# A fused retention and two-MLP kernel on one core: k and v of the first chunks on ScalarE's DMA queue, head and visits reordered, outputs in the next first bank

## The chip, the cores and the metric

The kernel runs on one core of one Trainium2 chip. A core has a matrix engine (TensorE, PE in the rows; its weight loads are PEld), a vector engine (VectorE, DVE), an activation engine (ScalarE, ACT), GpSimd (POOL) and SyncE (SP), which here does nothing but issue DMAs. Every engine works through its own list of instructions in order and waits on semaphores for the others. ScalarE can issue DMAs too. Data come from device memory into SBUF (128 partitions); matmuls write PSUM banks, which VectorE and ScalarE read. The metric is device time in microseconds, taken as the median of several runs. A profiled execution gives a span, from its first to its last instruction.

## The reference

Three stages on 4 sequences of 576 tokens, 8 heads of 64: a retention (attention without softmax, with a decay by head), then a softplus MLP and a squared-ReLU MLP, both 512 to 2048 to 512.

```
scores = (1/sqrt(D)) * q @ k^T
gamma  = 1 - 2.0 ** (-5 - arange(H))
ret    = scores * where(rel >= 0, gamma ** rel, 0)      # rel = i - j
x      = (ret @ v) -> [B*S, H*D]                         # 2304 x 512
h = x @ w_in;  g = max(h,0) + log1p(exp(-|h|));  x = g @ w_out
h = x @ w_in2; r = max(h,0); g = r*r;            out = g @ w_out2
```

All of it is float32.

## The kernel before, in words

**Retention by chunks.** The tokens are cut into 18 chunks of 64 positions of two sequences each (128 tokens). A chunk has one SBUF tile `ch`: its lower 64 partitions hold q and k by dimension, its upper 64 hold k and v by token, so each chunk comes in by transfers that write 64 partitions each (`load_chunk`). For a chunk, `scale_v` weights v with the decay. `step_s` then runs 32 matmuls for the scores (`pb`) and, interleaved, 32 for the running state (`st`), VectorE masks the scores back into `ch` (L355), and ScalarE copies the state into the next chunk's tile (L362). `step_o` runs 32 matmuls for the output (`po`), and VectorE multiplies it with weights `xw` into x (L393). For the first token tile ScalarE rounds x to `xh` (L400) and VectorE takes the rest `xl` (L401), since float32 matmuls are made of rounded parts: `ph` sums xh·wi and xl·wi.

**The MLPs.** Tokens go in five tiles (`TILES`, 512, 384, 512, 512, 384). A tile has 16 steps: g1 (12 matmuls into `ph`, L446), the softplus on ScalarE and VectorE (last line L473), and two steps later g2 (12 matmuls into `acc`, L498). `ph` alternates between two PSUM banks. Weights arrive as raw words through three staging buffers and are converted by ScalarE (L142, L143, L175) and VectorE (L147, L176) during the first tile. The later chunks of the retention are done in *visits* between steps (`attend`): output of chunk c−1, load of chunk c+1, scores and state of chunk c, scale of chunk c+1. In a visit before the change `po` has a bank of its own, and `pb` is put into the bank that the next `ph` takes. The second MLP (L592, L611) follows on six accumulators a batch, whose results are stored by two DMAs each, lower and upper partitions apart (L510).

**What sets the order.** The head, up to the first MLP, is in the order in which it is written (`tc.manual_schedule()`): loads first, then chunk by chunk, with dummy matmuls (`cold`, `keep_warm`) between. After it a scheduler merges the work of steps, visits and conversions, so the order on each engine is seen only in its list. All input DMAs stand on SP.

Of the kernel before, what the change touches and what calls it, by code (L numbers as in the profile page):

```python
# [43 lines left out]
def kernel(  # L44
# [74 lines left out]
    def load_w(src, kind, f):  # L119
        t = stage.tile([P, DM, 2], U32, tag="st", name=f"{kind}_raw")  # L120
        if kind == "wi":
            nc.sync.dma_start(
                out=t.rearrange("p (k m) two -> p k (m two)", k=KD),
                in_=src[:, f * P:(f + 1) * P].rearrange("(k p) m two -> p k (m two)", p=P),
            )
        else:
            nc.sync.dma_start(out=t, in_=src[f * P:(f + 1) * P])
# [114 lines left out]
    def pump_load(upto):  # L242
        while n_load[0] < min(upto, len(loads)):
            load_w(*loads[n_load[0]])
            n_load[0] += 1
# [52 lines left out]
    def new_chunk(c):  # L298
        if c < NPR:
            pool = first_pool if c < n_first else at  # L300
            chunk[c] = pool.tile([P, 3, 2, H, CN], F32, tag="ch", name="ch")

    def load_qk(c):
        if c < NPR:
            if c not in chunk:
                new_chunk(c)
            for s in range(2):
                nc.sync.dma_start(out=chunk[c][LO, 0:2, s], in_=qk_t[place(c, s)])

    def load_kv(c):  # L310
        if c < NPR:
            for s in range(2):
                nc.sync.dma_start(out=chunk[c][HI, 1:3, s], in_=kv[place(c, s)])

    def load_chunk(c):
        load_qk(c)
        load_kv(c)

    def scale_v(c, eng=nc.vector):
        if c < NPR:  # L320
            t = chunk[c][HI, 2]
            w = cst[HI, C_VW + c % SCH * H:C_VW + (c % SCH + 1) * H]
            eng.tensor_tensor(  # L323
                out=t, in0=t, op=ALU.mult,
                in1=w.unsqueeze(1).unsqueeze(3).to_broadcast([CN, 2, H, D]),
            )
# [7 lines left out]
    def step_s(c, pb):  # L334

        qp, kk, sv = (chunk[c][:, i] for i in range(3))
# [23 lines left out]
        if go_on:  # L360
            for of, i in ((LO, 0), (HI, 1)):
                nc.scalar.copy(chunk[c + 1][LO, 2, :, i * HH:(i + 1) * HH], st[of])  # L362

    def pb_acc():
        return ps_acc.tile([P, H, CN], F32, tag="at", name="pb")

    def step_o(c, ps):
        qkv = chunk.pop(c)
        qp, sv = qkv[:, 0], qkv[:, 2]
        rows = slice(0, P) if c % SCH else HI  # L370
        xw = xw_first if c % SCH == 0 else xw_now
        xw = xw.rearrange("p (a b) -> p a b", a=KD).unsqueeze(1).to_broadcast([P, 2, KD, CN])
        po = ps.tile([P, H, CN], F32, tag="at", name="po").rearrange(
            "p (s a) b -> p s a b", s=2
        )
        if c % SCH:
            make_xw(c % SCH)
# [54 lines left out]
    def pb_next():  # L432
        return h_bank("pb", False).rearrange("p (h c) -> p h c", c=CN)
# [68 lines left out]
    def drain_one(j, src, dsts, n):  # L502
# [6 lines left out]
        for rows, dst in dsts:  # L509
            nc.sync.dma_start(out=dst, in_=o[rows])  # L510
# [216 lines left out]
    nc.scalar.preload_act_table_set("natural_log_exp_and_others")  # L727
# [29 lines left out]
    def make_xw(m):  # L757
# [3 lines left out]
            out=xw_now.rearrange("p (a b) -> p a b", a=KD),  # L761
# [5 lines left out]
    with tc.manual_schedule():  # L767
# [24 lines left out]
        for c in range(last + 1):  # L792
            scale_v(c, nc.vector if c == last - 1 else nc.gpsimd)
            if c < last:
                keep_warm(1)
                step_s(c, pb_acc())
                if c:
                    step_o(c - 1, ps_acc)
                for _ in range((0, 0, 1, 2)[c]):
                    pump_step()  # L800
# [5 lines left out]
    step_s(last, pb_acc())  # L806
    tick[0] = last + 1
# [141 lines left out]
```

## Time and profile before

| what | us |
|---|---|
| median of 3 runs (885.42 to 886.35) | 885.65 |
| profiled execution, own time | 886.12 |
| its span | 884.4 |
| TensorE busy | 848.1 (96%) |
| VectorE busy | 577.6 (65%) |
| ScalarE busy | 421.8 (48%) |
| mean granted TensorE clock | 0.979 |

The time is a little longer than the span, since starting and ending lie outside of it. TensorE is busy 96% of the span, so the kernel is bound by it over most of its length; a share over the whole span says nothing on the stages at its two ends, where TensorE waits. In the page's rows a group reads: line, engine, operation, output from input, count, then busy time, mean of one, and the idle time just before with what ended it.

### The profile page before, as it was taken

The page shows a single profiled execution, that of the slowest core. Times are in us where ns is not written, and L with a number is a line of the kernel's source. Part 1 is how long each engine was busy: PE and PEld are TensorE (multiplying, and loading weights), DVE is VectorE, ACT ScalarE, POOL GpSimd, SP SyncE. Part 2 cuts the span into 40 slices and gives each one's busy share as a digit, 9 for nine tenths or more (in the row PEclk, how much of TensorE's full clock was granted, in tenths as well). Part 3 has the DMA queues.
Part 4 walks back from the last instruction along what each step waited for, and adds up shares of the span by engine and source line. Part 5 has one row for each costly group of instructions (what it writes and reads, how often), then busy time and mean ns, then how long its engine had stood idle before and what let it go on. Part 6 is the DMA issues. An engine that isn't in the chain of part 4 may idle for free.

```text
span 884.4 us, 14178 instructions
## 1 busy us (share of the span) xinstructions
PE 848.1 (96%) x5512; PEld 744.7 (84%) x5512; DVE 577.6 (65%) x974; ACT 421.8 (48%) x759; POOL 8.2 (1%) x8
## 2 busy tenths in 40 slices
PE   6699989999999999999999999999999999999996
PEld 5678778899877888788999989889888889998885
DVE  1689889886798668854888874547644445544543
ACT  2579889675577445744686461213322113221121
POOL 2100000000000000000000000000000000000000
PEclk7799999999999999999999999999999999999999
DMA  9776685883288106900431374346644344634343
GB/s 194 179 205 198 175 179 161 234 267 109 49 239 239 41 8 176 311 2 1 163 118 54 124 237 118 117 120 190 190 116 116 115 120 119 191 119 110 118 119 72
DMA packets 80678, 126.32 MB, mean 143 GB/s; under 512 B 7010, under 2 KB 41954, under 8 KB 80610
## 3 DMA queue, kind: packets, MB, share of 16 engines
q1 hardware_dynamic: 80612, 125.42, 50.9%
q8 instruction: 44, 0.72, 0.3%
q14 instruction: 22, 0.18, 0.1%
HBM read 101.28 MB, written 24.12 MB: 142 GB/s over the span
## 4 chain that ended last, share of the span: by engine, by line
PE 65%; DMA 12%; DVE 12%; ACT 7%; issue 2%; SPq 2%; DVEq 0%; ACTq 0%
PE acc L611 22%; PE ph L446 12%; PE acc L498 9%; PE py L592 8%; DMA ch<-in_kv_dram 7%; PE px L592 6%; PE pz L592 6%; DMA wi_raw<-in_moe_w_in_dram 3%; DMA wo_raw<-in_moe_w_out_dram 2%; DVE ct L147 2%; DVE e L473 1%; DVE l L470 1%; DVE e L467 1%; DVE ch L323 1%; DVE ch L355 1%
## 5 line engine op out<-in xcount | busy, mean ns | idle before, releaser
L446 PE MATMUL ph<-xh,wi 128*128 128x512 f32 (+1 forms) x640 | 152.1, 380 | 12.3 <-DVE ch L355 6.2
L446 PEld LDWEIGHTS ph<-xh,wi 128*128 128x128 f32 x640 | 118.6, 193 | 34.3 <-issue 5.0
L498 PE MATMUL acc<-gh,woh 128*128 128x512 f32 (+1 forms) x320 | 118.7, 372 | 0.0
L498 PE MATMUL acc<-gl,woh 128*128 128x512 f32 (+1 forms) x320 | 117.9, 368 | 0.0
L498 PE MATMUL acc<-gh,wol 128*128 128x512 f32 (+1 forms) x320 | 117.8, 368 | 0.0
L611 PE MATMUL acc<-woh,gring 128*128 128x512 f32 x288 | 104.9, 393 | 0.0
L592 PE MATMUL py<-t,sring 128*128 128x384 f32 x432 | 86.9, 335 | 0.3 <-DVE uring L703 0.3
L482 ACT CAST gh<-e 128x512 fp32r<-128x512 f32 (+1 forms) x80 | 46.0, 575 | 78.6 <-DVE e L473 72.5
L592 PEld LDWEIGHTS py<-t,sring 128*128 128x128 f32 x432 | 77.2, 188 | 6.8 <-DVE uring L703 0.6
L446 PE MATMUL ph<-xl,wi 128*128 128x512 f32 (+1 forms) x320 | 79.5, 369 | 0.0
L467 DVE SCALAR_TENSOR_TENSOR e<-e 128x512 f32<-128x512 f32 (+1 forms) x80 | 50.9, 636 | 37.4 <-ACT l L462 36.8
L483 DVE TENSOR_TENSOR gl<-e,gh 128x512 fp32r<-128x512 f32 (+1 forms) x80 | 50.9, 636 | 27.6 <-ACT gh L482 27.4
L498 PEld LDWEIGHTS acc<-gh,woh 128*128 128x128 f32 x320 | 60.0, 188 | 8.1
L498 PEld LDWEIGHTS acc<-gl,woh 128*128 128x128 f32 x320 | 60.1, 188 | 7.7 <-DVE gl L483 0.3
L498 PEld LDWEIGHTS acc<-gh,wol 128*128 128x128 f32 x320 | 60.1, 188 | 7.7
L446 PEld LDWEIGHTS ph<-xl,wi 128*128 128x128 f32 x320 | 59.5, 190 | 8.1
L641 ACT CAST gh<-g 128x384 fp32r<-128x384 f32 x48 | 24.6, 513 | 87.3 <-DVE g L628 72.6
L641 ACT CAST gring<-g 128x384 fp32r<-128x384 f32 x48 | 24.6, 513 | 80.1 <-DVE g L628 80.1
L460 ACT ACTIVATE e<-ph 128x512 f32<-128x512 f32 (+1 forms) x80 | 44.1, 552 | 38.6 <-PE ph L446 38.3
L611 PEld LDWEIGHTS acc<-woh,gring 128*128 128x128 f32 x288 | 54.0, 188 | 9.2
L592 PE MATMUL px<-t,sring 128*128 128x384 f32 x288 | 58.4, 337 | 0.0
L592 PE MATMUL pz<-t,sring 128*128 128x384 f32 x288 | 58.2, 337 | 0.0
(80 smaller groups left out, 1427.3 us busy)
## 6 DMA issues: line engine op xcount, KB each, us to landing
sring<-s2d SPq DMA_DIRECT2D x168, 256.0 KB, 2.7
wi_raw<-in_moe_w_in_dram SPq DMA_DIRECT2D x32, 512.0 KB, 4.8
wo_raw<-in_moe_w_out_dram SPq DMA_DIRECT2D x32, 512.0 KB, 4.6
s2d<-ct SPq DMA_DIRECT2D x48, 256.0 KB, 3.3
ch<-in_qk_t_dram SPq DMA_DIRECT2D x36, 256.0 KB, 4.9
ch<-in_kv_dram SPq DMA_DIRECT2D x36, 256.0 KB, 6.0
raw<-x2d SPq DMA_DIRECT2D x12, 384.0 KB, 3.4
out_dram<-xo SPq DMA_DIRECT2D x36, 128.0 KB, 2.4
```

The source lines that it names most:

```text
L147: nc.vector.scalar_tensor_tensor(out=ct, in0=up, scalar=3, in1=low, op0=ALU.logical_shift_left, op1=ALU.bitwise_or,)
L323: eng.tensor_tensor(out=t, in0=t, op=ALU.mult, in1=w.unsqueeze(1).unsqueeze(3).to_broadcast([CN, 2, H, D]),)
L355: nc.vector.tensor_tensor(out=qp[HI, :, i * HH:(i + 1) * HH], in0=pb[of].rearrange("p (s h) c -> p s h c", s=2), in1=mask[of].rearrange("p ...
L446: nc.tensor.matmul(ph[:, :n], lhsT=a, rhs=x, start=(j == 0), stop=(j == len(todo) - 1))
L460: nc.scalar.activation(out=e, in_=ph[:, :n], func=AF.Abs)
L467: nc.vector.scalar_tensor_tensor(out=e, in0=e, scalar=-2.0, in1=e, op0=ALU.add, op1=ALU.mult)
L482: nc.scalar.copy(h[:, :n], g)
L483: nc.vector.tensor_tensor(out=l[:, :n], in0=g, in1=h[:, :n], op=ALU.subtract)
L498: nc.tensor.matmul(acc[j][:, :n], lhsT=a, rhs=x, start=(begin and m == 0), stop=(end and m == 2))
L592: nc.tensor.matmul(ps, lhsT=a, rhs=x, start=(first and m == 0), stop=(m == len(todo) - 1), skip_group_check=True,)
L611: nc.tensor.matmul(acc2[j, m], lhsT=a, rhs=x, start=(begin and n == 0), stop=(end and n == 2))
L641: nc.scalar.copy(h, g)
```

## The change

1. *Queues in the head.* `load_w`, `pump_load` and `load_chunk` can issue on another queue. k and v of chunks 0 to 3 and the first weight block are issued by ScalarE, the rest of the head by SP. The table load of ScalarE moves behind its first DMA.
2. *Chunk tile.* It is laid out sequence by sequence, so one DMA brings q and k (or k and v) of both sequences, 512 KB, in pieces of 4 KB; before, two DMAs of 256 KB in pieces of 2 KB.
3. *Order in the head.* The weight blocks are loaded ahead of chunk 4; GpSimd scales all five of the head's chunks, in two instructions each; the output weights of chunks 1 to 3 are made early (`xw_soon`); the state copies become a call of their own (`next_state`); chunk 4's `step_s` moves into the first visits, of which the first tile now has four.
4. *Visits.* Scores first, into the bank that `po` had; the output of the chunk before goes into the bank of the next `ph` (`in_next`).
5. *Outputs.* The two stores of a result go one on SP and one on ScalarE.

```diff
+    def load_chunk(c, kv_queue=nc.sync):
...
+            at_c = slice(place(c, 0), place(c, 1) + 1, SCH)
+            nc.sync.dma_start(
+                out=chunk[c][LO, :, 0:2], in_=qk_t[at_c].rearrange("s p i h c -> p s i h c")
+            )
+            kv_queue.dma_start(
+                out=chunk[c][HI, :, 1:3], in_=kv[at_c].rearrange("s p i h c -> p s i h c")
+            )
...
-        for rows, dst in dsts:
-            nc.sync.dma_start(out=dst, in_=o[rows])
+        for queue, (rows, dst) in zip((nc.sync, nc.scalar), dsts):
+            queue.dma_start(out=dst, in_=o[rows])
...
-        load_chunk(0)
+        load_chunk(0, nc.scalar)
+        nc.scalar.preload_act_table_set("natural_log_exp_and_others")
...
-        for c in range(1, last + 1):
-            load_chunk(c)
-            if c == last - 2:
-                pump_load(1)
-            elif c == last - 1:
-                pump_load(3)
+        load_chunk(1, nc.scalar)
+        pump_load(1, nc.scalar)
+        load_chunk(2, nc.scalar)
+        load_chunk(3, nc.scalar)
+        pump_load(3)
+        load_chunk(last)
...
+        for c in range(last):
+            scale_v(c, nc.gpsimd)
+            keep_warm(2)
+            step_s(c, in_acc("pb"))
+            next_state(c)
+            if c:
+                step_o(c - 1, in_acc("po"))
+            for _ in range((0, 1, 2, 0)[c]):
+                pump_step()
         keep_warm(2)
-        step_o(last - 1, ps_acc)
-        keep_warm(6)
+        step_o(last - 1, in_acc("po"))
+        keep_warm(4)
+        scale_v(last, nc.gpsimd)
...
+            if b == 0:
+                before, n = before - 1, n + 1
...
                 c = tick[0]
-                step_o(c - 1, ps_at)
+                if c < NPR:
+                    step_s(c, ps_at.tile([P, H, CN], F32, tag="at", name="pb"))
+                if c - 1 in chunk:
+                    step_o(c - 1, in_next("po"))
                 load_chunk(c - 1 + LOADS)
                 if c < NPR:
-                    step_s(c, pb_next())
+                    next_state(c)
                 scale_v(c - 1 + LOADS)
```

What moves, engine by engine. First the loads of the head. On SP before, the first twelve transfers after the constants' rows (`ch` is a chunk, `cst` the masks and decay weights; L308 loads q and k, L313 k and v):

```order
L308 DMA ch<-in_qk_t_dram 64x2x512 x2
L313 DMA ch<-in_kv_dram 64x2x512 x2
L776 DMA cst<-in_consts_dram 64x138 x2
L308 DMA ch<-in_qk_t_dram 64x2x512 [waits DMAHW0_49]
L308 DMA ch<-in_qk_t_dram 64x2x512 [waits DMAHW1_49]
L313 DMA ch<-in_kv_dram 64x2x512 [waits DMAHW2_49]
L313 DMA ch<-in_kv_dram 64x2x512 [waits DMAHW3_49]
```

On SP now, up to chunk 4 (L308 q and k, L311 k and v, L122 a weight block):

```order
L308 DMA ch<-in_qk_t_dram 64x2x1024
L781 DMA cst<-in_consts_dram 64x138 x2
L308 DMA ch<-in_qk_t_dram 64x2x1024 [waits DMAHW0_49]
L308 DMA ch<-in_qk_t_dram 64x2x1024 [waits DMAHW2_49]
L308 DMA ch<-in_qk_t_dram 64x2x1024 [waits DMAHW4_49]
L122 DMA wi_raw<-in_moe_w_in_dram 128x4x256 [waits DMAHW5_49]
L122 DMA wi_raw<-in_moe_w_in_dram 128x4x256 [waits DMAHW6_49]
L308 DMA ch<-in_qk_t_dram 64x2x1024 [waits DMAHW7_49]
L311 DMA ch<-in_kv_dram 64x2x1024 [waits DMAHW0_49]
```

And on ScalarE now, from its start; before, its first row was the table load and its second the copy of the constants' rows:

```order
L311 DMA ch<-in_kv_dram 64x2x1024
L779 ACT_TABLE_LOAD
L311 DMA ch<-in_kv_dram 64x2x1024
L122 DMA wi_raw<-in_moe_w_in_dram 128x4x256
L311 DMA ch<-in_kv_dram 64x2x1024 [waits DMAHW1_49]
L311 DMA ch<-in_kv_dram 64x2x1024 [waits DMAHW3_49]
L757 COPY cst<-rows 128x256 [waits PE_49]
L361 COPY ch<-st 64x2x256 [waits PE_49]
```

The upper halves of chunks 0 to 3 left SP's list. A DMA that waits for a DMA semaphore waits for the landing of the last transfer that used it, which can be one of the other queue.

Second, VectorE ahead of the first `ph` (`ct` and `wi` are weight conversions, `ch<-pb` a mask, `x<-po` the output product). Before, from the `xl` of chunk 2:

```order
L401 TENSOR_TENSOR xl<-x,xh 128x2x4x64 [waits Activation_49]
L147 SCALAR_TENSOR_TENSOR ct<-wi_raw 128x512 [waits DMAHW0_49]
L147 SCALAR_TENSOR_TENSOR ct<-wi_raw 128x512 [waits DMAHW5_49]
L147 SCALAR_TENSOR_TENSOR ct<-wi_raw 128x512 [waits DMAHW6_49]
L176 TENSOR_TENSOR wi_393<-ct,wi_393 128x512 [waits Activation_49]
L760 SCALAR_TENSOR_TENSOR xw_now<-cst 128x256
L355 TENSOR_TENSOR ch<-pb,cst 64x2x256 [waits PE_49]
L393 TENSOR_TENSOR x<-po,xw_now 128x512 [waits DVE_49]
L355 TENSOR_TENSOR ch<-pb,cst 64x2x256
```

Now, from the `xl` of chunk 1 to the x of chunk 3:

```order
L404 TENSOR_TENSOR xl<-x,xh 128x2x4x64 [waits Activation_49]
L147 SCALAR_TENSOR_TENSOR ct<-wi_raw 128x512 [waits DMAHW6_49]
L147 SCALAR_TENSOR_TENSOR ct<-wi_raw 128x512 [waits DMAHW5_49]
L147 SCALAR_TENSOR_TENSOR ct<-wi_raw 128x512 [waits DMAHW6_49,Activation_49]
L176 TENSOR_TENSOR wi_331<-ct,wi_331 128x512 [waits Activation_49]
L352 TENSOR_TENSOR ch<-pb,cst 64x2x256 [waits PE_49]
L352 TENSOR_TENSOR ch<-pb,cst 64x2x256
L396 TENSOR_TENSOR x<-po,xw_soon 128x512 [waits PE_49]
L176 TENSOR_TENSOR wi_331<-ct,wi_331 128x512 [waits Activation_49] x2
L404 TENSOR_TENSOR xl<-x,xh 128x2x4x64 [waits Activation_49]
L396 TENSOR_TENSOR x<-po,xw_soon 128x512 [waits PE_49]
```

The masks here were chunk 4's and are now chunk 3's; chunk 4's come behind. On TensorE chunk 4's state matmuls still stand ahead of the first `ph`, but no longer its output matmuls.

Third, a visit in the second tile, on VectorE (`xr` is x of a later tile, `gl` and `e` softplus, the 128x256 `ct` a weight conversion). Before:

```order
L393 TENSOR_TENSOR xr<-po,xw_now 128x512 [waits PE_49]
L483 TENSOR_TENSOR gl<-e,gh 128x384 [waits Activation_49]
L467 SCALAR_TENSOR_TENSOR e<-e 128x384 [waits Activation_49]
L210 TENSOR_TENSOR ct<-ct 128x256 [waits DVE_49]
L470 SCALAR_TENSOR_TENSOR l<-e,l 128x384 [waits DVE_49]
L355 TENSOR_TENSOR ch<-pb,cst 64x2x256 [waits PE_49]
L355 TENSOR_TENSOR ch<-pb,cst 64x2x256
L473 SCALAR_TENSOR_TENSOR e<-ph,l 128x384 [waits DVE_49]
```

Now:

```order
L185 TENSOR_TENSOR ct<-ct 128x512 [waits DMAHW2_49,Activation_49]
L352 TENSOR_TENSOR ch<-pb,cst 64x2x256 [waits PE_49]
L352 TENSOR_TENSOR ch<-pb,cst 64x2x256
L396 TENSOR_TENSOR xr<-po,xw_now 128x512 [waits PE_49]
L470 SCALAR_TENSOR_TENSOR e<-e 128x384 [waits Activation_49]
L185 TENSOR_TENSOR ct<-ct 128x512 [waits DMAHW4_49,Activation_49]
```

The two masks stand ahead of the output's product, with nothing between; what is last of a visit to leave the next `ph`'s bank is the product and not the masks.

## Rows read from the trace of the kernel before

**Rows 1.** Five stages: busy time by engine, then clock, DMA share, GB/s.

```profile
0.00:44.29 44.29, 29.90 (x530) 26.49 (x530) 18.94 (x28) 16.11 (x28) 8.16 (x8) 0.74 0.85 186
44.29:148.50 104.21, 98.06 (x623) 78.45 (x623) 88.63 (x141) 90.23 (x159) 0.00 (x0) 0.95 0.71 188
148.50:500.00 351.50, 343.43 (x2492) 302.33 (x2491) 268.49 (x453) 217.64 (x389) 0.00 (x0) 1.00 0.44 129
500.00:876.30 376.30, 376.01 (x1869) 337.23 (x1868) 200.76 (x355) 97.28 (x185) 0.00 (x0) 1.00 0.48 137
876.30:884.40 8.10, 0.68 (x4) 0.22 (x2) 0.74 (x2) 0.59 (x1) 0.00 (x0) 0.81 0.74 170
```

**Rows 2.** Chain of waits through the head: start us, us, what.

```profile
17.99 15.43 DMA wi_raw<-in_moe_w_in_dram
...
36.51 0.69 DVE xl L401
37.20 3.52 DVE ct L147 x3
...
44.36 4.91 PE ph L446 x12
```

**Rows 3.** DMA issues of the first 40 us: count, KB, us to landing.

```profile
ch<-in_qk_t_dram SPq DMA_DIRECT2D x12, 256.0 KB, 7.7
ch<-in_kv_dram SPq DMA_DIRECT2D x10, 256.0 KB, 8.4
wi_raw<-in_moe_w_in_dram SPq DMA_DIRECT2D x3, 512.0 KB, 14.3
```

**Rows 4.** Stretches with different transfers, columns as in rows 1.

```profile
3.50:4.00 0.50, 0.50 (x5) 0.50 (x4) 0.00 (x0) 0.00 (x0) 0.00 (x0) 1.00 1.13 401
...
12.00:17.00 5.00, 3.56 (x89) 3.02 (x92) 1.38 (x2) 1.16 (x2) 1.90 (x1) 0.50 1.07 212
...
26.00:28.00 2.00, 0.00 (x0) 0.00 (x0) 0.69 (x1) 1.64 (x3) 0.00 (x0) 1.00 1.08 326
...
47.00:50.00 3.00, 3.00 (x29) 2.26 (x27) 0.69 (x1) 0.67 (x3) 0.00 (x0) 0.75 1.06 373
```

**Rows 5.** Timeline of the head: scales on GpSimd, first state matmuls of two chunks.

```profile
9.89 1.90 POOL L323 TENSOR_TENSOR ch<-ch,cst 64x1024 f32<-64x1024 f32 x1 [9.45 <-DMA cst<-in_consts_dram]
...
11.85 0.37 PE L350 MATMUL st<-ch 64*64 64x64 f32 x2 [5.02 <-POOL ch L323]
...
16.40 0.37 PE L350 MATMUL st<-ch 64*64 64x64 f32 x2 [1.44 <-POOL ch L323]
...
36.72 2.25 POOL L323 TENSOR_TENSOR ch<-ch,cst 64x1024 f32<-64x1024 f32 x1 [15.45 <-DMA ch<-in_kv_dram]
```

**Rows 6.** Waits after 44 us: us in total, times, longest.

```profile
ACT wo_raw L142 <- DMA wo_raw<-in_moe_w_out_dram: 12.9, 10, 3.5
...
PE ph L446 <- DVE ch L355: 6.2, 8, 1.2
PE ph L446 <- DVE e L473: 6.0, 5, 2.6
```

**Rows 7.** The tail: stretch, store issues, the last copy, landing times.

```profile
876.00:882.00 6.00, 0.98 (x5) 0.48 (x3) 1.04 (x2) 0.59 (x1) 0.00 (x0) 0.95 0.89 206
...
874.23 7.54 SPq L510 DMA_DIRECT2D out_dram<-xo  x12
...
878.53 0.69 DVE L508 COPY xo<-acc 128x512 f32<-128x512 f32 x1 [2.18 <-DMA out_dram<-xo]
...
out_dram<-xo SPq DMA_DIRECT2D x12, 128.0 KB, 2.4
```

**Rows 8.** First middle group of stores: a cast, its matmul; the ring's loads.

```profile
631.47 0.51 ACT L641 CAST gh<-g 128x384 fp32r<-128x384 f32 x1 [0.17 <-DVE g L628]
...
632.25 0.39 PE L611 MATMUL acc<-woh,gh 128*128 128x512 f32 x1
...
sring<-s2d SPq DMA_DIRECT2D x168, 256.0 KB, 2.7
```

More of the change, by code (lines that the diff above doesn't have):

```diff
@@ L126, in load_w @@
         else:
-            nc.sync.dma_start(out=t, in_=src[f * P:(f + 1) * P])
+            queue.dma_start(out=t, in_=src[f * P:(f + 1) * P])
         staged[kind, f] = t
@@ L240, with pump_load @@
     n_used = [0]
-    def pump_load(upto):
+    def pump_load(upto, queue=nc.sync):
         while n_load[0] < min(upto, len(loads)):
-            load_w(*loads[n_load[0]])
+            load_w(*loads[n_load[0]], queue)
             n_load[0] += 1
@@ L300, in new_chunk @@
             pool = first_pool if c < n_first else at
-            chunk[c] = pool.tile([P, 3, 2, H, CN], F32, tag="ch", name="ch")
-    def load_qk(c):
+            chunk[c] = pool.tile([P, 2, 3, H, CN], F32, tag="ch", name="ch")
+    def load_chunk(c, kv_queue=nc.sync):
         if c < NPR:
@@ L306, in load_qk @@
                 new_chunk(c)
[L307 to L317, printed above, removed]
+            at_c = slice(place(c, 0), place(c, 1) + 1, SCH)
[5 more added lines that the diff above has]
+            )
     def scale_v(c, eng=nc.vector):
         if c < NPR:
-            t = chunk[c][HI, 2]
             w = cst[HI, C_VW + c % SCH * H:C_VW + (c % SCH + 1) * H]
[L323 to L326, printed above, removed]
+            for s in range(2) if eng is nc.gpsimd else (slice(0, 2),):
+                t = chunk[c][HI, s, 2]
+                w_s = w.unsqueeze(2)
+                if len(t.shape) == 4:
+                    w_s = w_s.unsqueeze(1)
+                eng.tensor_tensor(out=t, in0=t, in1=w_s.to_broadcast(list(t.shape)), op=ALU.mult)
     state = []
@@ L334, in step_s @@
     def step_s(c, pb):
-        qp, kk, sv = (chunk[c][:, i] for i in range(3))
+        qp, kk, sv = (chunk[c][:, :, i] for i in range(3))
         go_on = c % SCH < SCH - 1
@@ L359, in step_s, with next_state, in_acc, step_o @@
             )
-        if go_on:
+    def next_state(c):
+        if c % SCH < SCH - 1:
             for of, i in ((LO, 0), (HI, 1)):
[L362 to L367, printed above, removed]
+                nc.scalar.copy(
+                    chunk[c + 1][LO, :, 2, i * HH:(i + 1) * HH], state[0][of]
+                )
+    def in_acc(name):
+        return ps_acc.tile([P, H, CN], F32, tag="at", name=name)
+    def step_o(c, po):
         qkv = chunk.pop(c)
-        qp, sv = qkv[:, 0], qkv[:, 2]
+        qp, sv = qkv[:, :, 0], qkv[:, :, 2]
         rows = slice(0, P) if c % SCH else HI
-        xw = xw_first if c % SCH == 0 else xw_now
-        xw = xw.rearrange("p (a b) -> p a b", a=KD).unsqueeze(1).to_broadcast([P, 2, KD, CN])
[L373 to L377, printed above, removed]
+        if c % SCH == 0:
+            xw = xw_first
+        elif c < n_first:
+            xw = xw_soon[:, c - 1]
+        else:
+            xw = xw_now
+            make_xw(xw, c % SCH)
+        xw = xw.rearrange("p (a b) -> p a b", a=KD).unsqueeze(1).to_broadcast([P, 2, KD, CN])
+        po = po.rearrange("p (s a) b -> p s a b", s=2)
         for s in range(2):
@@ L839 @@
         softplus_a(j, n)
-        if j == 0:
-            for c in range(last + 1, last + LOADS):
-                load_chunk(c)
-                scale_v(c)
         if j >= 1:
```

28 lines of the change are left out of this document (10 added, 18 removed).

## Prediction

> **What bounds the kernel now.** I read the table of stages first, then the chain of waits, then the DMA views. [rows 1] cut the span at four moments: the first matmul of the first MLP (44.29 us), the end of its first tile (148.5), the start of the second MLP (500), and the last matmul (876.3). From 500 on TensorE is busy 376.01 of 376.3 us, and from 148.5 to 500 all but 8: nothing is to be won there except at waits. What is left is the head (44.29 us, TensorE busy 29.90, much of it warm-up matmuls and half clock), the first tile (idle 6.15 of 104.21) and a tail of 8.1 us without matmuls.
>
> The chain through the head [rows 2] is DMA up to 33.42 (the last piece alone begins at 17.99) and then a string of short ScalarE and VectorE work up to the first `ph` matmul. So the head is bound by bytes: chunks 0 to 4 take 20 transfers of 256 KB (5.24 MB) and the first three weight blocks 1.57 MB [rows 3]. [rows 4] tell why 6.8 MB take so long. While only chunk halves move (12 to 17 us; each goes to 64 of the 128 partitions) the DMA engines are busy all the time, yet move 212 GB/s; while weight blocks move, which go to 128 partitions, they are just as busy and move 326 and 373. A single half transfer with empty queues ran at 401 GB/s for half a microsecond (3.5 to 4 us) and fell to 212 afterwards. I read this as a limit on the side of the 64 partitions, behind a buffer, and not as one of the engines or of memory. At 212 and 326 GB/s the head's bytes need 24.7 + 4.8 = 29.5 us; begun at about 3 us that is 32.5, and the chain leaves its last weight block at 33.42.
>
> **The change part by part.**
>
> *Two queues in the head.* q and k (lower half) stay on SP, k and v (upper half) of chunks 0 to 3 and the first weight block go through ScalarE's queue. If the limit is on the half, both halves now fill at once. I take 340 GB/s, between the two weight rows. ScalarE's queue holds 4 × 0.52 + 0.52 = 2.62 MB, SP's 4.19; until the first is empty 5.24 MB move in 15.4 us. SP then has a weight block left (0.52 MB, 1.5 us) and q, k and k, v of chunk 4, which are on one queue and follow each other at 212 GB/s (4.9 us). From 2.5 us that makes 24.3; SP's second q, k waits for the first k, v to land, a hole in one half of perhaps 1 us: chunk 4 lands at 25, not 36.72 [rows 5]. Scaling it takes GpSimd 1.9 to 2.25 us [rows 5], and by the new order TensorE does its state matmuls ahead of the first `ph`: not before 27.5.
>
> The compute in the head is the later of the two. Chunk 0's scale waited for the mask constants until 9.89 [rows 5]; they now stand behind one 512 KB transfer of SP, about 1.05 MB of both queues, so about 6. The scale is cut in two, the state matmuls start after its first half, at 7 (11.85 before). Chunk to chunk then took 4.55 us where data was nearly there (16.40 − 11.85); three of these put chunk 3's at 20.7. From there the order on VectorE decides: from the `xl` of chunk 1 at about 21 stand twelve instructions (three `ct`, three `wi`, two masks, x of chunks 2 and 3, two `xl`) of some 0.65 us (3.52 for three `ct`, 0.69 for `xl`, [rows 2]), 7.8 us, and then ScalarE's cast of chunk 3, 0.6: the first `ph` at 29.5, I take 30. **Term: −14.3 us.** Bounds: −16.8 (27.5, if VectorE's string is no later than the data) and −7.3 (no more than today's rates, worked out in the first rival).
>
> ScalarE pays four issues of about 0.63 us (SP's twelve took 7.54, [rows 7]) in front of its first copy, which is idle time now. Its third and fourth issue wait for the first loads to land; behind them stand the copies of the constants, then chunk 0's state copies, which cannot start before 8. Covered; if the fourth waited until 9, a microsecond.
>
> *First tile.* It moves as a block: g1 and g2 have the same matmuls, and chunk 4's output, which stood partly ahead of it, is now done in the first visits, four of them and not three. Its conversions (ScalarE 90.23 of 104.21 us, VectorE 88.63, [rows 1]) are as many as before, and by the order one more weight block is half converted at its start. **Term: 0**, bounds −6 (all its idle time) and +7 (second rival).
>
> *Visits.* The masks' operand `pb` now has a bank of its own, and the output `po` takes the bank of the next `ph`. Before, `ph` waited 8 times for VectorE's masks, 6.2 us in all [rows 6], because `pb` held its bank, and the masks came late in VectorE's order. Now masks and x stand together: `po` is read 0.7 us after its masks, while the 12 g2 matmuls between it and the next `ph` run. **Term: −3**, half of it, since VectorE is 76% busy there and the 6.0 us of waits for e [rows 6] may grow; bounds −6 and +3. One instruction per chunk goes (x's weights for chunks 1 to 3 are made early), at nothing.
>
> *Outputs on two queues.* In the tail 12 stores of 128 KB need 7.54 us of issues on SP alone and move at 206 GB/s; the last copy waited 2.18 us for a buffer [rows 7]. With six on each queue the copy may run at 878, its two stores be issued side by side, and land 2.4 us later at 882: **−2**, bounds −5 and 0. In the middle groups ScalarE issues six stores among its casts. One of these ends only 0.27 us before the matmul that needs it [rows 8]; four issues of 0.6 us ahead of it, less ScalarE's idle time there, cost perhaps half a microsecond in each of two groups: **+1**, bounds 0 and what the last rival says.
>
> *Packets.* A chunk's q and k of one sequence now lie together in SBUF, so pieces of 4 KB replace 2 KB. Weight blocks with small pieces are as fast as those with large: nothing.
>
> **Sum.** −14.3 − 3 − 2 + 1 = −18.3. The profiled execution took 886.12 us (884.4 of it span), 0.5 above the median of 885.65, so 867.8 against the profile and 867.3 against the median: **868**.
>
> **Where a rule speaks against it.** The Trainium skill (DMA: Bandwidth & Descriptors, Rules for kernel authors) says that spreading DMAs over SP and ScalarE gains no bandwidth, since both run on the same 16 engines, and that two transfers to the two partition halves serialize; SBUF — State Buffer (Door 1) says that 64 partitions reach 8 of 16 ports, about 217 GB/s, and that two transfers cannot be fused to reach all. The 212 GB/s agree with the second; of two halves in flight from two queues no row here shows anything. By the first rule the head keeps its rate and the time is that of the first rival.
>
> **Rivals.**
>
> 1. *The queues only take turns.* For: the DMA share is full at 212 GB/s, and SP's waits for landings of the other queue couple them. Against: the same engines move 326 to 373 when both halves are addressed. Then chunk 4 lands at 32.5, as worked out above, and the weights 4.9 us before it, at 27.6, since chunk 4 is now loaded last. ScalarE's two operations on the third block take 1.4 us; the `ct` and what follows on VectorE 7.1, the cast 0.6: the first `ph` at about 37, −7.3. The tail gains nothing: −7.3 − 3 + 1, **876**.
>
> 2. *The first tile gives it back.* For: its weights arrive through three staging buffers, ScalarE waited 12.9 us for `wo` loads alone after 44 us [rows 6], and it is 87% busy. A tile that starts 14 us earlier with late weights would be longer by up to half of that: −18.3 + 7, **874 to 877**. Against: the order has the same weights converted ahead of the first `ph`.
>
> 3. *Slower: ScalarE's stores hold its casts in the second MLP.* Each of the 12 middle stores waits for an earlier DMA on the same semaphore, often a weight load, which lands 2.7 us after its issue [rows 8]; TensorE has no idle time there to cover it. All 12 at 2.7 us are 32 us: 868 − 1 + 32, **899**. It ends slower than before once a store stalls TensorE by more than 1.6 us on average. Against: most of those DMAs are long landed, and a group of casts has buffers ahead.
>
> **How the numbers follow.** The forecast has 0.68, with 861 to 875 of its own; the first rival 0.17, the second 0.09, the third 0.04, and 0.02 that gains and losses cancel. Within 0.2% of 885.65 (1.8 us), what such a measurement can tell from no change, only the last falls: faster 0.94, same 0.02, slower 0.04. The range of 860 to 880 holds the first three.
>
> **What would show it.** Right: over 300 GB/s between 5 and 15 us, chunk 4's scale at 25, the first `ph` at 30, the first tile again about 104 us long, hardly a wait of `ph` for a VectorE line of the visits, stores at over 300 GB/s at the end. Wrong: about 210 GB/s in the head, or a first tile of 110 us, or TensorE idle around the two middle groups of stores.

## The result, and the profile after

The changed kernel takes 878.28 us (median of 7 runs, 874.41 to 881.45), the kernel before, run beside it, 885.42 (881.25 to 886.35). The ratio is 0.9918, interval 0.9891 to 0.9946: faster by 7.1 us, where 17.7 were forecast (885.65 to 868). The profiled execution (876.0 us, span 874.2) is one of the quicker ones.

The five stages of the changed kernel (busy time of each engine, then clock, DMA share, GB/s), against [rows 1]:

```profile
0.00:42.40 42.40, 28.27 (x508) 25.00 (x508) 21.06 (x30) 16.77 (x29) 11.89 (x14) 0.76 0.87 213
42.40:141.80 99.40, 93.99 (x648) 75.37 (x649) 89.03 (x140) 91.12 (x160) 0.00 (x0) 0.98 0.70 197
141.80:500.00 358.20, 351.25 (x2536) 310.04 (x2535) 275.62 (x465) 218.52 (x393) 0.00 (x0) 1.00 0.44 132
500.00:868.20 368.20, 368.20 (x1827) 329.99 (x1826) 192.88 (x340) 93.67 (x178) 0.00 (x0) 1.00 0.45 134
868.20:874.20 6.00, 0.03 (x1) 0.00 (x0) 0.69 (x1) 0.58 (x1) 0.00 (x0) 0.76 0.62 192
```

The head fell from 44.3 to 42.4 us only, where 30 was forecast. The first tile is 4.8 us shorter and the last stage 1.4 (from the last matmul, which stood at 877.0 before). The chain of waits through the head (start, length, what) says what the first `ph` matmul now waits for:

```profile
2.22 11.87 DMA wi_raw<-in_moe_w_in_dram
...
14.11 16.28 DMA wi_raw<-in_moe_w_in_dram
...
30.41 0.67 ACT wi_raw L142
31.08 0.52 ACT xh L403
...
33.59 6.86 DMA wi_raw<-in_moe_w_in_dram
...
40.53 0.70 ACT wi_raw L142
...
41.25 0.58 ACT ch L361
41.83 0.53 ACT xh L403
...
42.40 3.03 PE ph L449 x12
```

The first weight block, on ScalarE's queue, needs 11.87 us, the third, on SP's, 16.28. The last cast of x (41.83) stands on ScalarE behind the conversion of the fourth `wi` block, whose load was issued at 33.59, when a staging buffer came free, and behind a copy of chunk 4's state (41.25), which waits for TensorE's state matmuls. In e8, the same program again, that conversion is early (37.83) and the copy alone holds the cast (42.08):

```profile
41.60 0.58 ACT L361 COPY ch<-st 64x512 f32<-64x512 f32 x1 [3.11 <-PE st L347]
```

Rates in the head, columns as above:

```profile
3.00:5.00 2.00, 2.00 (x13) 1.80 (x14) 0.00 (x0) 0.00 (x0) 0.00 (x0) 1.00 0.95 236
5.00:7.00 2.00, 1.90 (x20) 1.56 (x16) 0.00 (x0) 0.00 (x0) 0.00 (x0) 1.00 1.05 223
7.00:9.00 2.00, 0.00 (x0) 0.00 (x0) 0.00 (x0) 0.00 (x0) 0.00 (x0) 1.00 0.98 207
9.00:11.00 2.00, 0.00 (x0) 0.00 (x0) 0.00 (x0) 0.00 (x0) 0.00 (x0) 1.00 1.07 230
11.00:13.00 2.00, 0.46 (x8) 0.30 (x12) 0.84 (x1) 0.46 (x2) 1.20 (x2) 0.55 1.11 259
13.00:15.00 2.00, 1.95 (x60) 1.76 (x60) 2.00 (x3) 0.00 (x0) 2.00 (x2) 0.50 1.02 297
```

Until 11 us these are hardly more than the old 212 [rows 4]. The queues' own counts for these stretches show that one of them carries most of the bytes at a time (0.41 MB of ScalarE's queue against 0.07 of SP's from 3 to 5 us, 0.06 against 0.39 from 5 to 7, 0.34 against 0.07 from 7 to 9); only from 13 to 15, with about equal shares (0.27 and 0.33), do they reach 297. TensorE has nothing to do from 7 to 11 us, and then works at half clock. On GpSimd, the first and the last scale of the head, against 9.89 and 36.72 in [rows 5] (start, length, what, idle time and releaser):

```profile
11.80 4.60 POOL L323 TENSOR_TENSOR ch<-ch,cst 64x512 f32<-64x512 f32 x4 [11.36 <-DMA cst<-in_consts_dram]
...
33.32 2.55 POOL L323 TENSOR_TENSOR ch<-ch,cst 64x512 f32<-64x512 f32 x2 [8.56 <-DMA ch<-in_kv_dram]
```

The mask constants, forecast at 6, land at 11.8; chunk 4's k and v, forecast at 25, at 33.3. The waits of TensorE from 42 to 500 us answer to [rows 6]:

```profile
PE ph L449 <- DVE e L476: 6.0, 8, 2.0
PE ph L449 <- DVE xr L396: 3.7, 6, 0.9
PE po L383 <- DVE e L476: 1.8, 3, 0.9
```

The 6.2 us of waiting for the masks are gone; 3.7 for x (L396) and 1.8 of `po` have taken their place. In tiles 2 to 5 alone all waits of TensorE come to 8.0 us before and 6.8 now. In the tail SP issues six stores and not twelve [rows 7]:

```profile
865.48 5.26 SPq L513 DMA_DIRECT2D out_dram<-xo  x6
```

### The profile page after: what moved, and what is told of

Read it like the earlier page. It is cut to its first block, busy times and chain, and to the rows that moved or that the text cites. A ratio compares the mean times of both kernels' runs of the same rounds, so it can differ in the third digit from the quotient of the medians.

```text
span 874.2 us, 14111 instructions
## 1 busy us (share of the span) xinstructions
PE 841.7 (96%) x5516; PEld 740.4 (85%) x5516; DVE 579.3 (66%) x973; ACT 420.7 (48%) x759; POOL 11.9 (1%) x14
## 4 chain that ended last, share of the span: by engine, by line
PE 64%; DVE 12%; DMA 11%; ACT 10%; issue 2%; ACTq 0%; DVEq 0%
PE acc L614 23%; PE ph L449 11%; PE acc L501 10%; PE py L595 9%; DMA wi_raw<-in_moe_w_in_dram 6%; PE px L595 6%; PE pz L595 6%; DMA wo_raw<-in_moe_w_out_dram 4%; ACT e L463 2%; DVE l L473 2%; DVE e L470 2%; DVE e L476 2%; ACT l L465 1%; ACT e L464 1%; ACT gh L485 1%
## 5 line engine op out<-in xcount | busy, mean ns | idle before, releaser
L449 PE MATMUL ph<-xh,wi 128*128 128x512 f32 (+1 forms) x640 | 148.0, 373 | 11.4 <-DVE e L476 6.0
L449 PEld LDWEIGHTS ph<-xh,wi 128*128 128x128 f32 x640 | 116.3, 188 | 32.4 <-DVE e L476 8.4
L614 PE MATMUL acc<-woh,gl 128*128 128x512 f32 x144 | 57.2, 398 | 0.0
```

The costliest lines, as they stand in the source:

```text
L449: nc.tensor.matmul(ph[:, :n], lhsT=a, rhs=x, start=(j == 0), stop=(j == len(todo) - 1))
L614: nc.tensor.matmul(acc2[j, m], lhsT=a, rhs=x, start=(begin and n == 0), stop=(end and n == 2))
```

## Experiments

e1 to e16 were timed in five rounds beside the kernel before on the same chip, e5, the loads alone, excepted. The groups (e1 to e4, e6 to e8, e9 to e12, e13 and e14, e15 and e16) ran on different chips, so between groups the ratios are to be compared. The stages are those of one profiled execution each, in us: the head up to the first `ph` matmul, the first tile up to the first `ph` of the second, tiles 2 to 5 up to the start of the last g1, from there to the end of the last matmul, the tail.

| kernel | median | ratio (95%) | head | tile 1 | tiles 2–5 | MLP 2 | tail |
|---|---|---|---|---|---|---|---|
| before | 885.42 | 1 | 44.3 | 104.2 | 342.7 | 385.8 | 7.4 |
| changed | 878.28 | 0.9918 (0.9891–0.9946) | 42.4 | 99.4 | 340.9 | 385.5 | 6.0 |
| e8, the same again | 875.67 | 0.9910 (0.9874–0.9946) | 42.8 | 101.6 | 340.1 | 386.2 | 6.0 |
| e1 head on SP | 873.59 | 0.9851 (0.9805–0.9896) | 38.4 | 98.9 | 341.4 | 385.9 | 6.1 |
| e9, e1 again | 872.16 | 0.9861 (0.9830–0.9893) | 38.1 | 98.0 | 341.4 | 385.6 | 5.9 |
| e2 constants first | 881.70 | 0.9947 (0.9916–0.9978) | 45.7 | 99.4 | 342.8 | 386.0 | 6.1 |
| e3 before + two store queues | 882.57 | 0.9964 (0.9932–0.9996) | 44.2 | 101.6 | 341.8 | 385.7 | 5.6 |
| e4 visits as before | 876.67 | 0.9880 (0.9831–0.9928) | 39.8 | 95.9 | 342.3 | 385.9 | 5.8 |
| e6 queues apart | 874.61 | 0.9889 (0.9851–0.9928) | 44.0 | 99.3 | 341.1 | 385.8 | 5.7 |
| e7 chunk 4 early | 871.93 | 0.9857 (0.9825–0.9889) | 40.0 | 95.4 | 341.5 | 386.0 | 5.9 |
| e10 e1 + chunk 4 early | 874.77 | 0.9890 (0.9851–0.9929) | 36.7 | 99.6 | 341.8 | 385.8 | 5.9 |
| e11 e10 + visits as before | 882.20 | 0.9968 (0.9944–0.9992) | 39.4 | 109.0 | 342.3 | 385.4 | 6.6 |
| e12 e10 + k, v first | 878.44 | 0.9930 (0.9907–0.9952) | 38.8 | 98.7 | 343.4 | 385.5 | 6.1 |
| e13 whole chunks, first try | 883.76 | 0.9994 (0.9969–1.0018) | 39.9 | 99.9 | 349.7 | 386.2 | 5.9 |
| e14 e13 + chunk 4 early | 884.30 | 0.9992 (0.9966–1.0018) | 42.3 | 98.8 | 349.3 | 385.8 | 5.7 |
| **e15 whole chunks** | **863.54** | **0.9738 (0.9709–0.9766)** | 29.5 | 95.8 | 340.2 | 386.2 | 5.8 |
| e16 e15 + chunk 4 early | 868.67 | 0.9797 (0.9766–0.9828) | 29.0 | 96.9 | 345.5 | 385.7 | 5.7 |

The same program's head differs by 0.1 to 0.4 us between two executions and its first tile by 0.9 to 2.6 (the changed kernel and e8, e1 and e9; before and e3 share theirs too). Smaller differences of one execution prove nothing.

**e1 and e9: the second queue undone.**

```diff
-        load_chunk(0, nc.scalar)
+        load_chunk(0)
...
-        load_chunk(1, nc.scalar)
-        pump_load(1, nc.scalar)
-        load_chunk(2, nc.scalar)
-        load_chunk(3, nc.scalar)
+        load_chunk(1)
+        pump_load(1)
+        load_chunk(2)
+        load_chunk(3)
```

> The changed kernel with all loads of the head on SP's queue again, in the same order in the program. Theory (in the first 12 us the two queues only took turns at about 210 GB/s, so the second queue brought little): the last of chunk 4 lands between 32 and 35 us, the first ph matmul is at 41 to 45 us (42.4 with two queues), the time within 2 us of the changed kernel. Rival (where both queues ran together, at 13 to 20 us, they moved 290 GB/s, and this is worth some microseconds): with one queue the loads end 3 to 4 us later, at 36 to 37, the first ph at 46, the time 3 to 4 us above the changed kernel. Third (ScalarE was the one that lost, its copies of the constants waiting behind an issue until 11.67): the first ph before 40 and a time below 876.

> The kernel with all loads of the head on SP once more, beside its variants. By its first run: 1.5% below the kernel before (1.0 to 2.0), the first ph at 38 to 40. If the gain over two queues was chance, it is the 0.9% of the changed kernel and the first ph is past 41.

My theory missed on its own number, and the third rival's numbers came out: one queue is better by 4 us of head, in both pairs. With it chunk 0's v is scaled from 9.88 and not 11.80, and ScalarE copies its constants at 5.72, not 11.67 behind four issues; that this copy was the cause is not shown: e6 has it at 5.92 and no shorter head. The bytes come at the old rate, but more in the order in which they are needed; with two queues at the same total rate, the first transfers of each come at a share of it. TensorE waits 5.5 us for q and k in the head of the changed kernel and not at all in e1, and it stops there for 3.8 us with no releaser, against 1.6. Yet the scales of chunks 2 and 3 come later in e1 (20.89 and 27.01, against 18.35 and 22.27), and chunk 4's state matmuls, which stand ahead of the first `ph` in the changed kernel (from 37.6), stand behind it in e1 (41.4). How much of the 4 us belongs to which of these is open. The first scale of e1:

```profile
9.88 2.05 POOL L323 TENSOR_TENSOR ch<-ch,cst 64x512 f32<-64x512 f32 x2 [9.44 <-DMA cst<-in_consts_dram]
```

**e2, e3 and e4: one part each.** e2 moves the two `cst` loads ahead of `load_chunk(0, nc.scalar)`; e3 is the kernel before with the edit of `drain_one`; e4 puts `po` back into its own bank, ahead of the load, and `pb` into the next `ph` bank.

> The changed kernel with the two loads of the mask constants moved ahead of chunk 0's q and k on SP. Theory (the last waits of the head are those for the third and fourth weight blocks, not for chunk 0's scale): GpSimd scales chunk 0 from about 9 us and not 11.8, the state matmuls of chunks 0 and 1 come 1 to 3 us earlier, and the first ph matmul stays within 1 us of 42.4; the time within 1 us of the changed kernel. Rival (the whole string of short work starts late because of the constants, and the rest follows it): the first ph 3 to 5 us earlier, 38, and the time 3 to 5 us lower, 874.

> The kernel before with one edit: of the two stores of each output tile one goes through ScalarE's queue. Theory (the tail gains what the trace of the changed kernel shows, 1.4 us, and the middle stores cost nothing): the tail from the last matmul to the end 6.0 us and not 7.4, the time 884.2 (-0.16%). Rival (ScalarE's stores hold its casts in the second MLP): TensorE idle by 0.5 to 2.7 us around the middle stores, the time equal to the kernel before or above it.

> The changed kernel with the visits' order and banks as before: the output of the chunk before into its own bank and first, the masks' operand in the bank of the next ph. Theory (the visits are what shortened the first tile and the next ones): ph waits for VectorE's masks again, 6 us in all, the first tile is 2 to 5 us longer than 99.4 and the stretch behind it 2 us longer, the time 4 to 7 us above the changed kernel. Rival (the first tile gained from the weights converted ahead of it and from starting with more work done): the first tile within 1 us of 99.4, and the time at most 2.5 us above the changed kernel.

e2: the constants came at 9.03, as expected, but the head ended at 45.7: neither theory. Chunk 2's k and v, issued by ScalarE at 6.5, landed at 25.4 only; they stood in its queue behind the first weight block, which landed 16.4 us after its issue at 6.02, while most of the bytes went through SP's queue (1.07 MB of 1.35 from 12 to 18 us). e3: the stores gain 0.4% (0.04 to 0.7), nothing stalls in the middle. e4: no slower than the changed kernel, so its theory fell; tiles 2 to 5 alone are 1.4 us longer.

**e5, e6: the rate by itself, and the queues kept from waiting for each other.** e6 makes the two row loads one, and:

```diff
-        pump_load(1, nc.scalar)
         load_chunk(2, nc.scalar)
         load_chunk(3, nc.scalar)
         pump_load(3)
```

> All computation is left out: only transfers, in six stretches with a barrier between them. Loads of 512 KB: lower and upper halves in turn on SP's queue; lower halves on SP and upper ones on ScalarE's queue; lower halves on both queues; weight blocks of 128 partitions on SP; weight blocks on both. Then stores of 128 KB: 18 on SP, 18 on both queues in turn. Theory (one half takes about 210 GB/s, and two queues give more only while each has a half of its own in flight): 210 GB/s on SP alone, 290 to 300 with a half on each queue, 210 with both queues on the lower half, 350 to 370 for weight blocks on one queue or two; stores 206 alone and 250 to 300 on both. Rival (two queues share one stream, and what ran at 290 in the kernel was a remnant of weight blocks among the halves): 210 to 220 with a half on each queue too, and stores the same on one queue as on two.

> The changed kernel with its two queues kept from waiting for each other at the start: the two row loads are one transfer, and all three weight blocks of the head come through SP behind chunk 3, so that SP issues chunk 1's q and k, and ScalarE all four k and v, without a wait for a chunk's landing. Theory (the head term failed because an issue on one queue waits for a landing on the other, so that mostly one half was in flight until 12 us): 280 to 300 GB/s from 4 us on, chunk 3 landed at 18 to 20 us (k and v 22.3 in the changed kernel), ScalarE's copies of the constants at 5 and not 11.67, the first ph at 34 to 37, the time 5 to 7 us below the changed kernel. Rival (the half in flight does not matter, the two queues take turns whatever is issued): 210 GB/s until 20 us and the first ph at 40 or later, no gain. Second rival (with the weights behind chunk 3, VectorE's string waits for them): 290 GB/s, but the first ph at 40 or later.

The stretches of e5 (columns: VectorE, GpSimd, clock, DMA share, GB/s), in the order of the expectation; the second stretch in two pieces:

```profile
14.00:23.00 9.00, 3.76 (x5) 0.00 (x0) 1.00 1.03 219
27.00:33.00 6.00, 0.15 (x1) 0.00 (x0) 1.00 1.03 236
34.00:42.00 8.00, 0.15 (x1) 0.00 (x0) 1.00 1.03 269
48.00:66.00 18.00, 0.92 (x6) 0.00 (x0) 1.00 1.03 209
71.00:82.00 11.00, 0.98 (x7) 0.00 (x0) 1.00 1.09 354
88.00:97.00 9.00, 0.92 (x6) 0.00 (x0) 1.00 1.10 353
102.00:112.00 10.00, 1.46 (x3) 0.00 (x0) 1.00 0.88 203
118.00:124.00 6.00, 0.00 (x0) 0.00 (x0) 1.00 0.93 292
```

In this one execution two queues with a half each in flight move 236 GB/s for the first 6 us and 269 later, against 219 on one queue: 8 to 23% more, and not 60%. In the first of these stretches the queues share unequally (0.86 and 0.56 MB), in the second equally (1.08 each). Both on one half stay at 209, so the half is a limit; only a transfer to all 128 partitions reaches 354, on one queue as on two. Stores do gain, 203 to 292, but not by reaching more of SBUF at once: on one queue SP issues them back to back, 18 in 11.48 us, and 131 KB every 0.64 us is 205 GB/s; each lands 2.3 to 2.4 us after its issue began, the last like the first. So one queue was bound by its issues, which two queues divide between them. The Trainium skill (DMA: Bandwidth & Descriptors, Rules for kernel authors) says of two transfers to the two halves that they serialize, and to use one of 128 partitions; the loads here agree in part (236 to 269 against 219), and for the single transfer fully (354). e6 shows the same within the kernel, from 5 to 15 us with both queues loaded:

```profile
5.00:7.00 2.00, 2.00 (x13) 1.55 (x12) 0.58 (x2) 0.46 (x2) 0.00 (x0) 1.00 1.07 225
7.00:9.00 2.00, 1.90 (x9) 1.60 (x8) 0.52 (x2) 0.00 (x0) 0.00 (x0) 1.00 0.99 209
9.00:11.00 2.00, 0.16 (x2) 0.16 (x4) 0.00 (x0) 0.00 (x0) 0.00 (x0) 1.00 1.07 222
...
13.00:15.00 2.00, 0.14 (x4) 0.14 (x8) 0.00 (x0) 0.00 (x0) 1.24 (x2) 1.00 1.02 285
```

So the waits between the queues did not keep the rate down: the rival holds up to 11 us. From 13 to 17, with about equal shares of the two queues, halves alone move 285 and 291 GB/s, still under the 340 of the prediction. The constants landed later still, at 13.7. The head of 44.0 does not speak of the rate alone: e6 also put the first weight block behind chunk 3, and TensorE stopped three times in it with no releaser, for 7.4 us in all.

**e7, e8, e10: chunk 4's step.** e7 does `step_s(last)` and `next_state(last)` in the head again, takes out the extra visit, and loads and scales chunk 5 behind the first g1. e8 is the changed kernel unaltered, e10 is e7 with e1's loads.

> The changed kernel with chunk 4's step ahead of the first MLP tile and chunk 5's load and scale behind its first g1, as in the kernel before; two queues and the visits' order as changed. Theory (the first tile became shorter, 104.2 to 99.4, since VectorE no longer stands in the middle of its conversions before chunk 5's late k and v): the first tile 101 to 104 us, VectorE waits 1 to 4 us for chunk 5's k and v, the time 2 to 4 us above the changed kernel. Rival (the gain comes from more weights converted ahead and a higher clock): the first tile within 1.5 us of 99.4, the time that of the changed kernel within 2 us.

> The changed kernel unaltered, beside the others on the same chip: to see how far its head moves from one execution to the next. All theories: a time 0.8% below the kernel before, within its interval of 0.5 to 1.1%; the first ph between 39 and 43 us.

> All loads of the head on SP, and chunk 4's step ahead of the first tile. Theory (taking chunk 4's step out of the first visits helped the changed kernel because there the last cast of x stood behind the fourth weight block's conversion in ScalarE's order; with all loads on SP that cast already stands ahead of it): the same time as with all loads on SP alone, within 2 us. Rival (chunk 4's step among the first visits costs by itself, in the first tile): 3 to 4 us less than with all loads on SP alone, the first tile 95 to 96 us and not 99.

My theory for e7 fell: the tile did not grow, and the time is 3.7 us under e8's (the intervals overlap a little). On ScalarE of e7 the last cast of x comes right behind the conversion of the first `wo` block, ahead of that of the fourth `wi` block:

```profile
36.30 0.77 ACT L143 ACTIVATE wo_raw<-wo_raw,cst 128x512 uint32<-128x512 uint16 x1
38.18 0.62 ACT L403 CAST xh<-x 128x512 fp32r<-128x512 f32 x1 [1.11 <-DVE x L396]
```

In the changed kernel it comes 3.5 us later, behind that conversion and a copy of chunk 4's state, which in e7 follows the cast (40.19). Part of this is not the order: VectorE's product, which the cast needs, is itself 2.8 us later there (40.30 against 37.46). In e8 the product comes at 38.32 and the cast at 42.08, held by the state copy and not by the conversion. So the order on ScalarE costs some 0.7 us in the one execution and 3 in the other, and the copy is what both have in common. With e1's loads the cast stands ahead already, and e10 gains nothing over e9 (2.6 us more, the intervals overlap), nearly as that theory said; e10's profile has a stop of ScalarE of 5.0 us in the first tile for which no releaser shows, which blurs it.

**e11, e12: the visits again, and k, v ahead of q, k.**

> The same with the visits' order and banks as in the kernel before. Theory (the new order of the visits takes away waits of ph, but gives them back as waits of po, and VectorE and ScalarE set the pace): the same time as with the new order, within 2 us. Rival (it is worth the 3 us of the prediction): 3 us more, over tiles 1 to 5.

> All loads of the head on SP, chunk 4's step ahead of the first tile, and k and v of each chunk loaded ahead of its q and k. Theory (the head is a string of transfers at 210 GB/s, and a chunk's scaling and state need only k and v): scales and state matmuls come up to 2.4 us earlier (512 KB at 210 GB/s), the first ph 1 to 2 us earlier than without this edit. Rival (VectorE's and ScalarE's string and the weights set the first ph): no change within 1 us.

In tiles 2 to 5 the visits' order is worth 0.5 us here (341.8 and 342.3). e11 as a whole is 7.4 us slower than e10, which neither theory had: it lost 9.4 us in its first tile, and with e4 the same edit lost nothing. Why is open: the scheduler deals out the tile's work anew at each edit. e12 was slower, neither theory.

**e13 to e16: the limit taken away.** A chunk comes in one transfer of 1 MB to 128 partitions, on SP. e15, against e1:

```diff
-            nc.sync.dma_start(out=chunk[c][LO, :, 0:2], in_=qk_t[at_c]...)
-            kv_queue.dma_start(out=chunk[c][HI, :, 1:3], in_=kv[at_c]...)
+            nc.sync.dma_start(out=chunk[c][:, :, 0:2], in_=qkvk[at_c]...)
...
-                t = chunk[c][HI, s, 2]
+                v, t = chunk[c][HI, s, 0], chunk[c][HI, s, 2]
...
-                eng.tensor_tensor(out=t, in0=t, in1=...)
+                eng.tensor_tensor(out=t, in0=v, in1=...)
```

`qkvk` is the same input laid out with q, k above v, k. e13 kept k, v in that order and so had to copy the state over the lower k between scores and state matmuls. e14 and e16 add e7's edit.

> All loads on SP, and a chunk's q, k, k and v come in one transfer of 1 MB to all 128 partitions: the lower half of the tile holds q and k, the upper one k and v; the state is then copied over the lower k and the masked product over the upper k, each once its reader is done. Theory (a half takes about 210 GB/s, 128 partitions take 350, so this is the gain that the two queues were to bring): over 330 GB/s in the head from 5 us on, chunk 4 landed at 22 to 25 us (33.3 in the changed kernel), GpSimd's last scale done by 28. What is left then is the string of casts on ScalarE and VectorE: the first ph at 30 to 34, a time 4 to 8 us below the kernel with all loads on SP (872). Rival (the head hangs on the string of short work and the fourth weight block's conversion, which stands ahead of the last cast of x here as in the changed kernel, whatever the rate): the loads end by 25, but the first ph at 37 or later and no gain over 872.

> The same, with chunk 4's step ahead of the first tile and chunk 5's load and scale behind its first g1, as in the kernel before. Theory (as above; chunk 4 lands early enough for its step to hide in the head): the first ph within 2 us of the kernel without this edit, the time within 3 us of it. Rival (its masks and copies lengthen the string before the first ph): the first ph 2 to 4 us later, and the time too.

> All loads on SP, a chunk in one transfer of 1 MB to all 128 partitions, without the flaw of the first try (there scores and state matmuls no longer interleaved, 3.9 us a chunk and not 2.1, and the state copy stood between them): the upper half is loaded as v and k in the places of q and k, and the scale writes v into the third place, so no matmul, mask or copy moves. Theory (late bytes and constants are what held TensorE's string of chunk steps in the head; the string itself is about 22 us of work): over 350 GB/s, constants landed at 7 as in the first try, the first state matmul at 8 to 9, the first ph at 30 to 34, the time 4 to 8 us below the kernel with all loads on SP, 864 to 868. Rival (the conversions of the weights and casts on VectorE and ScalarE hold the first ph, as they come out of three staging buffers): the first ph at 36 or later, and no more than 2 us gained.

> The same, with chunk 4's step ahead of the first tile and chunk 5's load and scale behind its first g1, as in the kernel before. Theory (its work was moved behind the first ph to no purpose): first ph 1 to 2 us later than without this edit, the first tile 2 to 4 us shorter, the time within 2 us. Rival (it lengthens the string before the first ph and gives nothing back): 2 to 4 us slower.

e13 brought all five chunks by 23 us and lost it: its state matmuls, 32 in 1.97 us, no longer interleave with the scores, and the copies stand between, in the head and in the visits (tiles 2 to 5 are 8 us longer than the others). At the same half clock (0.50 from 13 to 24 us, where e15 has 1.00) 32 scores and 32 state matmuls apart take 3.9 us, while the 64 together take 2.1 in the changed kernel (17.71 to 19.79). e14's head is 2.4 us later than e13's and its time the same. e15 has the bytes without that, and nearly the theory's numbers. Its stretches, columns as in the changed kernel's:

```profile
3.00:5.00 2.00, 2.00 (x11) 1.77 (x12) 0.00 (x0) 0.00 (x0) 0.00 (x0) 1.00 0.87 344
5.00:7.00 2.00, 2.00 (x13) 1.55 (x12) 0.55 (x2) 0.46 (x2) 0.00 (x0) 1.00 1.03 400
7.00:11.00 4.00, 4.00 (x77) 3.71 (x76) 2.00 (x4) 0.27 (x1) 3.81 (x4) 1.00 1.04 376
11.00:15.00 4.00, 3.48 (x116) 3.07 (x116) 2.84 (x5) 2.05 (x4) 1.91 (x3) 1.00 1.03 412
15.00:24.00 9.00, 5.68 (x194) 4.93 (x188) 6.67 (x11) 6.89 (x12) 3.75 (x4) 1.00 0.89 314
24.00:33.00 9.00, 9.00 (x125) 7.54 (x122) 8.58 (x13) 6.51 (x12) 1.14 (x2) 0.81 0.81 283
```

They have 344 to 412 GB/s up to 15 us, no idle gap on TensorE before its chunk steps, and full clock up to 24 us; after it, at a mean of 0.81, chunk 3's output matmuls take 1.91 us where chunk 2's took 1.11. On GpSimd, the first and last scales of the head:

```profile
7.19 4.46 POOL L319 TENSOR_TENSOR ch<-ch,cst 64x512 f32<-64x512 f32 x4 [6.76 <-DMA cst<-in_consts_dram]
...
23.09 2.05 POOL L319 TENSOR_TENSOR ch<-ch,cst 64x512 f32<-64x512 f32 x2 [3.81 <-DMA ch<-in_qkvk_dram]
```

And the end of its chain: TensorE's own string and no longer a load.

```profile
23.02 1.11 PE po L379 x32
24.14 1.15 PE cold L733 x4
25.29 1.91 PE po L379 x32
27.19 1.19 PE cold L733 x8
...
29.55 2.98 PE ph L445 x12
```

e15 is the fastest of all, 2.6% under the kernel before, e9 1.4%. With the bytes early e7's edit loses 5 us (e16), more than the rival's 2 to 4, and most of it in tiles 2 to 5; with late bytes it seemed to gain, in the head and the first tile (e7 against e8). Why tiles 2 to 5 grow is open.

## Why the prediction was wrong, point by point

- **The step that failed: "If the limit is on the half, both halves now fill at once. I take 340 GB/s, between the two weight rows."** The limit on the half is there (209 with both queues on one half), but two half transfers together move 236 to 269 by themselves, and in the kernel 207 to 236 until 11 us and at most 297 after. The two weight rows it was taken from are of single transfers to 128 partitions, and say nothing of two halves. So chunk 4 landed at 33.3 and not 25, and the head term was −1.9 and not −14.3, outside its bounds. The first rival, that the queues only take turns, was nearer: 876 forecast, with −7.3 of head. So by the prediction's own sums the rate is worth some 7.0 of the 12.4 us that the head term missed. The other 5.4 are not divided up: sharing the rate delayed the constants (11.8 for 6), TensorE waited 5.5 us for q and k, it stopped for 3.8 us with no releaser, and the order on ScalarE put a copy of chunk 4's state, and in one execution a late weight block, before the last cast; the prediction had none of these. That the time lies near this rival's 876, and inside the stated 860 to 880, is luck: its head gain did not come either, and the first tile, put at nothing, made up for part of it.
- **The string of short work in the head** (state matmuls of chunk 0 at 7, of chunk 3 at 20.7, first `ph` at 30) came out near, given the bytes: at 344 to 412 GB/s e15 has them at 8.9 and 18.6, and the first `ph` at 29.5. The path is another, so the good fit is in part luck: VectorE's string and a cast were to end the head, and in e15 TensorE's own matmuls do, slowed by a stop of 2.8 us and half clock after it.
- **ScalarE's issues**: the copies of the constants came at 11.67 and not by 9, but chunk 0's state matmuls began at 12.9 only, so the wait was covered, as said.
- **First tile, 0**: −4.8 in the first pair of executions and 0 between e8 and e3 (101.6 each); not settled beyond that scatter. The second rival, that the tile gives back what the head gains, did not happen: e15 gains 14.8 in the head and its tile is 95.8. (Of that rival's 874 to 877 only the 874 follows from its sum.)
- **Visits, −3**: the waits for masks went (6.2 us) and 5.5 us of others came; with the smaller ones tiles 2 to 5 wait 8.0 us before and 6.8 now. The new wait is the one for the output's product (3.7), which the prediction thought covered by g2; the waits for `e`, which it feared, stayed at 6.0. Tiles 2 to 5 show −1.8 against before, −1.4 against e4, and −0.5 between e10 and e11. Right in direction, too large.
- **Packets, nothing**: not tested by itself. Pieces of 4 KB to 128 partitions moved 412 GB/s (e15, 11 to 15 us), those of 1 KB 354 (e5), so their size may count for something.
- **Tail, −2**: −1.4, and e3 by itself −1.8 and 0.4% in time. The tail before was 7.4 us and not 8.1, since the last matmul ends at 877.0 and not at 876.3; the last copy still waits 1.95 us for a store, against 2.18. **Middle stores, +1**: 0; TensorE is busy 368.20 of 368.20 us there, so the third rival fell.
- The terms of the profile sum to −1.9 − 4.8 − 1.8 − 0.3 − 1.4 = −10.2; the second execution, e8, gives −1.5 − 2.6 − 2.6 + 0.4 − 1.4 = −7.7, nearer to the median's −7.1.

## What to carry to other kernels

Where loads are bound by the partitions they reach, as the halves were here, a second queue moved the bytes hardly faster and in a worse order; what helped was a layout in which one transfer reaches all 128 partitions. Take a rate for a sum only from a row of the very pattern you will run, and run that pattern alone first if no row has it. When bytes are early, look again at every order that was chosen while they were late.

## What the runs showed of the hardware

VectorE's `xw_soon` products take 3.34 us for three while GpSimd's scale runs beside them in the changed kernel, 1.95 in e8, where the scale begins halfway, and 1.10 in e1, where GpSimd is idle (first row the changed kernel, second e1):

```profile
12.16 3.34 DVE L764 SCALAR_TENSOR_TENSOR xw_soon<-cst 128x256 f32<-128x256 f32 x3 [11.10 <-ACT cst L757]
```

```profile
6.21 1.10 DVE L764 SCALAR_TENSOR_TENSOR xw_soon<-cst 128x256 f32<-128x256 f32 x3 [5.14 <-ACT cst L757]
```

TensorE and ScalarE stop now and then for 2 to 5 us with nothing to wait for that the profile shows, as here in chunk 2's step of the changed kernel; a packet of the queue q8, which the profile calls instruction, is under way in the same stretch (23.35 to 24.54), but that it is the cause no run shows:

```profile
26.09 0.37 PE L341 MATMUL pb<-ch 64*64 64x64 f32 x2 [2.72 <-issue]
```

In the changed kernel the chunk steps that follow 4 us of an idle TensorE ran at a granted clock of 0.50 (1.2 GHz); those of e15, which follow work without a gap, ran at 1.00 (2.4 GHz) up to 24 us and at a mean of 0.81 from 24 to 33, after a stop of 2.8 us. This is no rule: in e6 TensorE did next to nothing from 9 to 15 us and ran at 1.00 from 15 to 23. Why two queues with a half each share unequally at first, at 236 GB/s, and equally later, at 269, stays open.
